# Early transfer of the fourth chunk, a new order on VectorE at the outset, and weight conversion by halves in a fused retention and feed-forward kernel

## The chip, the cores and the metric

The kernel runs on one core of one Trainium2 chip. The metric is the device time of one execution in microseconds (us). A profiled execution gives a trace; its span, from the first to the last instruction, is 1.7 to 2.4 us shorter than the device time of the same run. Engines are called by their short names in the profile: PE is TensorE, PEld its weight loads, DVE is VectorE, ACT is ScalarE, SPq the queue that issues transfers. PSUM is the memory in which this kernel's matmuls leave their results.

## The reference, cut to what matters

```python
# retention: batch 4, 8 heads, 768 tokens, head size 64
state = gamma * state + k_t (outer) v_t
y_t = scale * q_t @ state
x = y as (3072 tokens, 512)
# feed-forward, w_in (512, 2048) and w_out (2048, 512) in 64-bit floats
h = x @ w_in
g = h * erf(softplus(h))
out = g @ w_out
```

The kernel does retention in chunks of 128 tokens (scores, mask, outputs, an addition to the state) and the feed-forward part in 32-bit floats. The weights come as 64-bit floats and are converted on the chip from their bits, piece by piece. There are 16 pieces of 1 MB; a piece of `w_in` serves two of the hidden blocks of the first 512 tokens.

## The kernel before

The first 512 tokens need four chunks. Then hidden blocks (g, u), with g the group and u the block in it, alternate with project(g), which multiplies the gated hidden values by `w_out`. Everything is emitted in program order, and in the traces each engine works through its own instructions in that order.

```python
def load(j):                      # k, q, v of chunk j
    KQ[j] = loads.tile([P, 2, H, D], F32, name="kq")     # pool of three
    V[j] = loads.tile([P, H, D], F32, name="v")
    ...

def conversion(n):                # piece n, five steps, one per yield
    ...
    nc.vector.tensor_scalar(power, hi, 0x7FF00000, None, op0=ALU.bitwise_and)      # mask
    nc.scalar.activation(power, power, AF.Relu, bias=below, scale=8.0)             # ScalarE
    yield
    nc.vector.tensor_scalar(number, hi, 0xFFFFF, 1 << 20, ...)
    yield
    nc.vector.scalar_tensor_tensor(numberf, number, 2.0**32, lo, ...)
    yield
    nc.vector.scalar_tensor_tensor(power, hi, 1 << 31, power, ...)   # needs the Relu
    load_pieces_after(n)
    yield
    nc.vector.scalar_tensor_tensor(to, numberf, 2.0**-52, power, ...)
    done.add(pieces[n])
    yield

def weights():                    # the order of all steps
    before = iter(())
    for n in range(n_p):
        now = conversion(n)
        if n > 1:                 # look ahead: mask and Relu of n before the rest of n - 1
            next(now)
            yield
        for _ in before:
            yield
        before = now
    ...

def pace(n):                      # room is a budget: one step for each unit
    room += n
    while room >= 1:
        next(weight_steps, None)
        room -= 1

def need(*what):                  # emit steps until this weight is there
    while what not in done:
        ...
        room -= 1

def hidden(g, u):
    ft = g * FG + u
    need("in", ft // 2)
    ...                                            # 4 matmuls (8 in the trace) into PSUM tile p
    nc.scalar.copy(HS[g][:, ...], p)               # ScalarE
    done.add(("hidden", ft))
    pace_around(3.4)                               # steps of the conversion come here
```

The gate of group g, two table loads and two activations over 2048 columns, is 6.4 us on ScalarE and follows hidden (g, 3).

## Time and profile before

| stage of the kernel before (span 694.0 us) | us | PE busy | DVE busy | granted PE clock |
|---|---|---|---|---|
| four chunks of retention, 0 to 33 | 33.0 | 25.83 | 16.92 | 0.95 |
| hidden blocks (0,0) to (1,3), 33 to 67 | 34.0 | 32.59 | 32.20 | 1.00 |
| project(0) to project(2), 67 to 140 | 73.0 | 73.00 | 60.11 | 1.00 |
| the remaining tokens, 140 to 694 | 554.0 | 548.40 | 274.59 | 1.00 |

Device time was 694.71 us when the prediction was made (three runs, 694.33 to 694.75). The profiled run took 695.74. The table is summed from windows of the trace: busy time of an engine in a stretch, and the share of its full clock that TensorE was granted. PE is full from 67 to 140 us, and the change is aimed at what lies before, so only the first two rows have something to give, 7.2 + 1.4 us of PE's idle time (the last row has 5.6 us more).

### The profile page before, as it was taken

To read this page: it belongs to the slowest core of one execution; us is meant where nothing else is said; L and a number is where in the kernel's file an instruction comes from. 1 tells how busy PE (TensorE), PEld (TensorE's weight loads), DVE (VectorE), ACT (ScalarE), POOL (GpSimd) and SP (SyncE) were. 2 spreads that over 40 slices of the span, in tenths; PEclk is the share of its full clock that TensorE was granted. 3 is DMA by queue.
4 is the path that set the end of the run, shared out by engine and by line. 5 is a ranking of instruction groups with operands and counts; after the bars stand their busy time and mean duration, and the time that the engine had idled before them with its cause. 6 is when DMAs were issued, how large, how long until landed. Compare 5 with 4: busy or idle time off the path is not lost.

```text
span 694.0 us, 14331 instructions
## 1 busy us (share of the span) xinstructions
PE 679.8 (98%) x6214; PEld 579.7 (84%) x6214; DVE 383.8 (55%) x581; ACT 257.2 (37%) x291; POOL 6.6 (1%) x21
## 2 busy tenths in 40 slices
PE   8799999999999999999999999999999999999997
PEld 7544454486999999999999999999999999999996
DVE  4599999364863663564455455544544554343323
ACT  3266453425244143243342341441441432432440
POOL 2000000010000000000000000000000000000000
PEclk9999999999999999999999999999999999999999
DMA  9999963102321231222222222322311200000000
GB/s 191 209 254 246 208 167 91 31 1 37 104 45 32 68 56 30 63 45 44 68 43 44 69 39 46 71 37 44 70 39 39 54 30 1 2 31 2 1 31 32
DMA packets 147216, 47.12 MB, mean 68 GB/s; under 512 B 135760, under 2 KB 136016, under 8 KB 147152
## 3 DMA queue, kind: packets, MB, share of 16 engines
q1 hardware_dynamic: 144640, 45.66, 30.0%
q8 instruction: 49, 0.80, 0.5%
q10 hardware_dynamic: 2512, 0.53, 0.5%
q14 instruction: 15, 0.12, 0.1%
HBM read 39.86 MB, written 6.29 MB: 67 GB/s over the span
## 4 chain that ended last, share of the span: by engine, by line
PE 91%; DVE 3%; DMA 2%; SPq 1%; issue 1%; ACT 0%; POOL 0%; DVEq 0%; POOLq 0%
PE hp L712 36%; PE o L784 35%; PE o L655 8%; PE hp L642 4%; DMA w_in_sb<-in_moe_w_in_dram 2%; PE r L520 1%; PE hp L485 1%; PE o L367 1%; PE o L556 1%; SPq L114 1%; DMA w_out_sb<-in_moe_w_out_dram 1%; DVE w_out_sb L211 1%; PE hp L535 1%; PE r L408 1%; PE r L535 1%
## 5 line engine op out<-in xcount | busy, mean ns | idle before, releaser
L712 PE MATMUL hp<-xs,w_in_sb 128*128 128x128 f32 x1280 | 149.8, 275 | 0.0
L712 PEld LDWEIGHTS hp<-xs,w_in_sb 128*128 128x128 f32 x1280 | 147.8, 192 | 1.6 <-issue 0.5
L784 PE MATMUL o<-w_out_sb,h 128*128 128x256 f32 x640 | 141.7, 379 | 0.0
L784 PEld LDWEIGHTS o<-w_out_sb,h 128*128 128x128 f32 x640 | 121.6, 190 | 16.5
L712 PE MATMUL hp<-xT,w_in_sb 128*128 128x128 f32 x960 | 113.7, 275 | 0.0
L712 PEld LDWEIGHTS hp<-xT,w_in_sb 128*128 128x128 f32 x960 | 111.9, 192 | 1.9 <-issue 1.0
L784 PE MATMUL o<-w_out_sb,e 128*128 128x256 f32 x480 | 112.1, 383 | 0.0
L631 DVE TENSOR_TENSOR e<-h,e 128x1024 f32<-128x1024 f32 x42 | 49.6, 1221 | 102.5 <-ACT e L612 102.5
L784 PEld LDWEIGHTS o<-w_out_sb,e 128*128 128x128 f32 x480 | 88.2, 190 | 11.6
L642 PE MATMUL hp<-xT,w_in_sb 128*128 128x512 f32 x128 | 56.5, 595 | 0.5 <-ACT xT L475 0.5
L737 DVE TENSOR_TENSOR h<-h,hp 128x512 f32<-128x512 f32 x20 | 13.8, 688 | 75.3 <-PE hp L712 75.3
L607 ACT ACT_TABLE_LOAD x24 | 30.8, 1283 | 60.8 <-issue 45.3
L642 PEld LDWEIGHTS hp<-xT,w_in_sb 128*128 128x128 f32 x128 | 23.9, 190 | 29.2 <-issue 28.2
L612 ACT ACTIVATE e<-e 128x2048 f32<-128x2048 f32 (+1 forms) x23 | 42.2, 1838 | 0.2
L607 ACT ACTIVATE e<-h 128x2048 f32<-128x2048 f32 x22 | 42.1, 1912 | 0.2
L725 DVE TENSOR_TENSOR h<-h,hp 128x512 f32<-128x512 f32 x20 | 13.8, 688 | 51.3 <-PE hp L712 51.3
L735 ACT COPY h<-hp 128x512 f32<-128x512 f32 x20 | 11.7, 587 | 60.2 <-PE hp L712 60.2
L730 ACT COPY h<-hp 128x512 f32<-128x512 f32 x20 | 11.7, 587 | 57.9 <-PE hp L712 57.9
L728 ACT COPY h<-hp 128x512 f32<-128x512 f32 x20 | 11.7, 587 | 55.3 <-PE hp L712 55.3
L612 ACT ACT_TABLE_LOAD x24 | 30.8, 1283 | 0.4
L574 ACT COPY xT<-r 128x256 f32<-128x256 f32 x32 | 10.5, 375 | 54.8 <-PE r L520 54.8
L723 ACT COPY h<-hp 128x512 f32<-128x512 f32 x20 | 11.8, 589 | 48.6 <-PE hp L712 48.6
(123 smaller groups left out, 676.5 us busy)
## 6 DMA issues: line engine op xcount, KB each, us to landing
w_out_sb<-in_moe_w_out_dram SPq DMA_DIRECT2D x14, 512.0 KB, 5.1
kq<-in_k_dram SPq DMA_DIRECT2D x24, 256.0 KB, 3.7
v<-in_v_dram SPq DMA_DIRECT2D x24, 256.0 KB, 3.1
w_in_sb<-in_moe_w_in_dram SPq DMA_DIRECT2D x12, 512.0 KB, 8.7
out_dram<-r SPq DMA_DIRECT2D x23, 256.0 KB, 3.3
kq<-in_q_dram SPq DMA_DIRECT2D x256, 16.0 KB, 1.8
kb<-in_k_dram SPq DMA_DIRECT2D x256, 16.0 KB, 1.7
w_out_sb<-in_moe_w_in_dram SPq DMA_DIRECT2D x4, 512.0 KB, 7.8
```

What stands on the lines that cost most here:

```text
L535: nc.tensor.matmul(other[a][own, u % 2, D:] if crossed else pp[a][own, u % 2, t], V[j][t, 2 * u + r, :], AM[j][t, r, u, :D], start=crossed ...
L607: nc.scalar.activation(E[g], HS[g], AF.Softplus)
L612: nc.scalar.activation(E[g][:, half], E[g][:, half], AF.Erf)
L631: nc.vector.tensor_tensor(E[g][:, half], HS[g][:, half], E[g][:, half], op=ALU.mult)
L642: nc.tensor.matmul(p, w_in_of(ft, kk), XC[0][:, kk, :], start=(kk == 0), stop=(kk == n_k - 1))
L655: nc.tensor.matmul(O[0][tt].rearrange("p (d c) -> p d c", d=2), E[g][:, u * TCH + tt * P : u * TCH + (tt + 1) * P], w_out_of(ft), start=(f ...
L712: nc.tensor.matmul(bank[:, u, :], w_in_sb[:, s, IN[a], kk, u * P : (u + 1) * P], XS[m][b][:, kk, :], start=(p in (1, 2, 5) and u == 0 and ...
L723: nc.scalar.copy(h["11"], flat)
L725: nc.vector.tensor_tensor(h["11"], h["11"], flat, op=ALU.add)
L728: nc.scalar.copy(h["12"], flat)
L737: nc.vector.tensor_tensor(h["12"], h["12"], flat, op=ALU.add)
L784: nc.tensor.matmul(O[m][i][:, half, :], G[g][a][:, u * P : (u + 1) * P], w_out_sb[:, s, OUT[b], u, :], start=i not in started, stop=(s == ...
```

## The change

It has three parts. The fourth chunk (j = 3) no longer waits for one of three buffers; its place is the tile of the first gate, which isn't written for a long time yet. VectorE scales the next chunk before it masks the present one now for the third chunk too (for the first two it did already), and hardly any weights are converted during the chunks. The first two pieces are converted in two halves each, so that the first hidden block needs half a piece only. Along with these, looking ahead starts later (`n > 3`), the budget starts at 0, and the fifth chunk's steps move one hidden block later.

```diff
 def load(j):
+    if j == JPC - 1:
+        x = act.tile([P, N], F32, name="e", bufs=1)     # the first gate's place
+        KQ[j] = x[:, : 2 * d_model]...
+        V[j] = x[:, 2 * d_model : 3 * d_model]...
+    else:
         ...
+    if j == JPC - 1:
+        load_piece(0)                                   # between q and v of chunk 3
...
 def conversion(n):
+    for part in range(2) if n < 2 else (None,):         # halves for pieces 0 and 1
         mask; Relu
-        yield
+        if part is None:
+            yield
         number
         yield
         ...
...
-            if n > 1:
+            if n > 3:
                 next(now)
                 yield
...
-load(1); load(2); load_piece(0)
+for j in range(1, JPC): load(j)
+for n in range(1, 4): load_piece(n)
...
 def hidden(g, u):
-    need("in", ft // 2)
+    need("in", ft)
...
+for j in range(JPC):
+    S_(j)                               # scores
+    if j + 1 < JPC: K_(j + 1)           # scale the next chunk
+    if j: A(j - 1)                      # state
+    if j + 1 < JPC: T(j + 1)            # transposes
+    else: next(weight_steps)
+    M(j)                                # mask
+    O_(j)                               # outputs
 early = False
+room = 0.0
```

More of the change, by code (lines that the diff above doesn't have):

```diff
@@ L101, in load @@
         b, c = divmod(j, NC)
-        KQ[j] = loads.tile([P, 2, H, D], F32, name="kq")
-        V[j] = loads.tile([P, H, D], F32, name="v")
+        if j == JPC - 1:
+            x = act.tile([P, N], F32, name="e", bufs=1)
+            KQ[j] = x[:, : 2 * d_model].rearrange("p (i h d) -> p i h d", i=2, h=H)
+            V[j] = x[:, 2 * d_model : 3 * d_model].rearrange("p (h d) -> p h d", h=H)
+        else:
+            KQ[j] = loads.tile([P, 2, H, D], F32, name="kq")
+            V[j] = loads.tile([P, H, D], F32, name="v")
         now = slice(c * C, (c + 1) * C)
@@ L139 @@
     raws = [x[:, : 2 * CE].bitcast(I64) for x in spare]
-    number = spare[0][:, 2 * CE :].bitcast(U32)
+    numbers = spare[0][:, 2 * CE :].bitcast(U32)
     powers = [x[:, 2 * CE :].bitcast(U32) for x in spare[1:3]]
@@ L169, in load_piece @@
                 )
-    held = []
     def load_pieces_after(n):
@@ L176, in load_pieces_after @@
             if place[later] == place[n]:
-                if early:
-                    held.append(later)
-                else:
-                    load_piece(later)
+                load_piece(later)
                 break
-    def load_held():
-        for n in held:
-            load_piece(n)
-        held.clear()
     def conversion(n):
         which, i = pieces[n]
-        words = raws[place[n]].bitcast(U32).rearrange("p (n w) -> p n w", w=2)
-        lo, hi = words[:, :, 0], words[:, :, 1]
@@ L195, in conversion @@
         half, s, at = i // 4, i % 4 // 2, i % 2
-        if which == "in":
-            to = w_in_sb[:, s, 2 * half : 2 * half + 2, :, at * 2 * P : (at + 1) * 2 * P]
-            form, sizes = "p (d k f) -> p d k f", dict(d=2, k=2)
-        else:
-            to = w_out_sb[:, s, 2 * half : 2 * half + 2, at * 2 : at * 2 + 2, :]
-            form, sizes = "p (d f c) -> p d f c", dict(d=2, f=2)
-        power = powers[n % 2]
-        nc.vector.tensor_scalar(power, hi, 0x7FF00000, None, op0=ALU.bitwise_and)
@@ L204, in conversion @@
-        nc.scalar.activation(power, power, AF.Relu, bias=below, scale=8.0)
-        yield
-        nc.vector.tensor_scalar(
-            number, hi, 0xFFFFF, 1 << 20, op0=ALU.bitwise_and, op1=ALU.bitwise_or
-        )
-        yield
-        numberf = number.bitcast(F32)
-        nc.vector.scalar_tensor_tensor(numberf, number, 2.0**32, lo, op0=ALU.mult, op1=ALU.add)
-        yield
-        nc.vector.scalar_tensor_tensor(
-            power, hi, 1 << 31, power, op0=ALU.bitwise_and, op1=ALU.bitwise_or
-        )
@@ L216, in conversion @@
-        load_pieces_after(n)
-        yield
-        nc.vector.scalar_tensor_tensor(
-            to,
-            numberf.rearrange(form, **sizes),
-            2.0**-52,
-            power.bitcast(F32).rearrange(form, **sizes),
-            op0=ALU.mult,
-            op1=ALU.mult,
-        )
-        done.add(pieces[n])
-        yield
+        for part in range(2) if n < 2 else (None,):
+            words = raws[place[n]].bitcast(U32)
+            if which == "in":
+                f = slice(at * 2 * P, (at + 1) * 2 * P)
+                if part is not None:
+                    f = slice((at * 2 + part) * P, (at * 2 + part + 1) * P)
+                to = w_in_sb[:, s, 2 * half : 2 * half + 2, :, f].rearrange("p d k f -> p (d k) f")
+            else:
+                to = w_out_sb[:, s, 2 * half : 2 * half + 2, at * 2 : at * 2 + 2, :].rearrange(
+                    "p d f c -> p d (f c)"
+                )
+            words = words.rearrange("p (a b w) -> p a b w", a=to.shape[1], w=2)
+            number, power = (
+                x.rearrange("p (a b) -> p a b", a=to.shape[1]) for x in (numbers, powers[n % 2])
+            )
+            if part is not None:
+                f = slice(part * P, (part + 1) * P)
+                words, number, power = words[:, :, f], number[:, :, f], power[:, :, f]
+            lo, hi = words[:, :, :, 0], words[:, :, :, 1]
+            nc.vector.tensor_scalar(power, hi, 0x7FF00000, None, op0=ALU.bitwise_and)
+            nc.scalar.activation(power, power, AF.Relu, bias=below, scale=8.0)
+            if part is None:
+                yield
+            nc.vector.tensor_scalar(
+                number, hi, 0xFFFFF, 1 << 20, op0=ALU.bitwise_and, op1=ALU.bitwise_or
+            )
+            yield
+            numberf = number.bitcast(F32)
+            nc.vector.scalar_tensor_tensor(numberf, number, 2.0**32, lo, op0=ALU.mult, op1=ALU.add)
+            if part is None:
+                yield
+            nc.vector.scalar_tensor_tensor(
+                power, hi, 1 << 31, power, op0=ALU.bitwise_and, op1=ALU.bitwise_or
+            )
+            if part != 0:
+                load_pieces_after(n)
+            yield
+            nc.vector.scalar_tensor_tensor(
+                to, numberf, 2.0**-52, power.bitcast(F32), op0=ALU.mult, op1=ALU.mult,
+            )
+            done.update((which, 2 * i + u) for u in (range(2) if part is None else (part,)))
+            yield
@@ L294 @@
     nc.scalar.copy(idle_out, ident[:, :1])
-    load(1)
-    load(2)
-    load_piece(0)
+    for j in range(1, JPC):
+        load(j)
+    for n in range(1, 4):
+        load_piece(n)
     causal = const.tile([P, C], F32, name="causal")
@@ L581, in sub_visit @@
             nc.vector.tensor_tensor(state, state, new[1], op=ALU.add)
-    def ret_loads(j):
-        if j == 0:
-            load(j + 3)
-        if j < 3:
-            load_piece(j + 1)
     def ret_add(j):
@@ L651, in project @@
             O[0] = [ps_o.tile([P, d_model], F32, name=f"o{i}") for i in range(TT)]
-        need("out", 2 * g + 1)
+        need("out", g * FG + FG - 1)
         for u in range(FG):
@@ L835 @@
     keep_warm(3)
-    n_first = JPC
-    for j in range(n_first):
+    for j in range(JPC):
         S_(j)
-        ahead = j < 2
-        if ahead:
+        if j + 1 < JPC:
             K_(j + 1)
+        if j:
+            A(j - 1)
+        if j + 1 < JPC:
             T(j + 1)
+        else:
+            next(weight_steps)
         M(j)
         O_(j)
-        if not ahead and j + 1 < n_first:
-            K_(j + 1)
-            T(j + 1)
-        ret_loads(j)
-        if j == 1:
-            A(j)
-            room = 1.0
-        pace(1)
-        if j != 1 and j + 1 < n_first:
-            A(j)
     early = False
-    load(JPC)
-    load_held()
-    waiting.append((A, n_first - 1))
+    room = 0.0
+    waiting.append((A, JPC - 1))
     after = [
-        [([], []), ([], []), ([], []), ([], [(K_, 4)])],
+        [([], []), ([(load, 4)], []), ([], []), ([], [])],
         [
-            ([(load, 5)], []),
+            ([(load, 5)], [(K_, 4)]),
+            ([], []),
             ([(T, 4)], []),
             ([(S_, 4)], [(M, 4)]),
-            ([(O_, 4), (load, 6)], [(A, 4), (K_, 5)]),
         ],
         [
-            ([], []),
+            ([(O_, 4), (load, 6)], [(A, 4), (K_, 5)]),
             ([(T, 5), (load, 7)], []),
```

## The prediction

> **What bounds the kernel now.** I read the page first (busy shares), then the windows, then the chain of waits up to 70 us, then the timelines of VectorE (DVE), ScalarE (ACT) and the DMA queue for the stretch in which TensorE (PE) is not full.
>
> The page and the windows (PE busy, PEld, DVE, ACT, POOL, granted clock, DMA share, GB/s):
>
> ```profile
> PE 679.8 (98%) x6214; PEld 579.7 (84%) x6214; DVE 383.8 (55%) x581; ACT 257.2 (37%) x291; POOL 6.6 (1%) x21
> ...
> 20.00:25.00 5.00, 2.33 (x44) 1.84 (x44) 4.97 (x7) 1.15 (x1) 0.00 (x0) 0.94 0.94 202
> 25.00:30.00 5.00, 3.82 (x44) 3.19 (x44) 2.56 (x4) 1.82 (x4) 0.00 (x0) 0.72 1.06 220
> ...
> 60.00:67.00 7.00, 5.62 (x57) 3.11 (x55) 6.93 (x9) 1.74 (x2) 0.00 (x0) 1.00 0.84 264
> 67.00:140.00 73.00, 73.00 (x221) 33.66 (x220) 60.11 (x64) 34.51 (x34) 0.00 (x0) 1.00 0.54 129
> ```
>
> PE idles 694.0 - 679.8 = 14.2 us in all, and from 67 to 140 us not at all. A faster outset can give at most a few us of 694; a new wait of PE in the first 140 us adds in full.
>
> Where the outset is lost (VectorE, then PE):
>
> ```profile
> 19.94 0.69 DVE L203 TENSOR_SCALAR w_out_sb<-w_out_sb 128x1024 uint32<-128x1024 uint32 x1
> ...
> 22.41 0.68 DVE L433 TENSOR_TENSOR am<-r,causal 128x512 f32<-128x512 f32 x1
> ...
> 24.74 1.22 DVE L393 TENSOR_TENSOR kq<-kq,kq_s 128x1024 f32<-128x1024 f32 x1
> ...
> 33.03 20.87 PE L642 MATMUL hp<-xT,w_in_sb 128*128 128x512 f32 x48 [0.47 <-ACT xT L475]
> ```
>
> The conversion of weight piece 0 goes ahead of the third mask (19.94 to 22.41), so PE stands still for 2.5 us (20.64 to 23.15); the clock is then 0.5 for 3.4 us (24.25 to 27.7 in half-us windows). The fourth chunk is scaled at 24.74, as its load was issued only when chunk 0's buffer came free (13.58). The hidden matmuls begin at 33.03 and run without a hole; project(0) begins at 67.01.
>
> The lines on which my prediction turns are these of ScalarE:
>
> ```profile
> 40.20 0.59 ACT L645 COPY h<-hp 128x512 f32<-128x512 f32 x1 [2.85 <-PE hp L642]
> 40.68 1.15 ACT L204 ACTIVATE w_in_sb<-w_in_sb,below 128x1024 uint32<-128x1024 uint32 x1
> ```
>
> VectorE's mask for that Relu ended at 40.26 and ScalarE had been idle 2.85 us, yet the Relu began only at 40.68, behind the copy of hidden block 1, because it stands behind it in the program. Here it costs nothing: it is for piece 3, two blocks early.
>
> **What the Trainium skill says.** (1) "PSUM — Partial Sum Buffer", section "Engine vs sequencer instructions": the queues of ScalarE and VectorE are strict FIFO. The two lines above agree (0.42 us of needless waiting). (2) "ScalarE: Activation LUTs", "What ACT_TABLE_LOAD costs": an ACTIVATE with a pointer bias takes about 280 ns + 0.833 ns per element: 1.13 us for 1024 (trace 1.15), so I take 0.71 for a half of 512. (3) "VectorE: DVE Perf Modes", "The TRN2 errata — SBUF-src ops pay a fixed extra latency per instruction": (N+151)/0.96 ns in fp32: 1.22 us for 1024 (trace 1.22), so 0.69 for 512. (4) "TensorE: Matmul & The Clock Gate", "What's actually happening": after an idle window of about 3.4 us TensorE gets half its clock. The trace agrees (0.5 for 3.4 us), and shows that a window with 28% PE work (0.94 of 3.4 us from 20.84) is idle enough.
>
> **The change part by part.**
>
> *Fourth chunk early.* The loads are the same bytes, no longer waiting for a buffer. Their order puts k and q of chunk 3 at 2.88 MB of the stream; by the windows (129, 220, 214, 199 GB/s) 2.8 MB are in at 15 us, so about 16 us, before VectorE wants it (16). Piece 0 ends at 3.9 MB (21 us), v at 4.2 (22), piece 1 at 5.2 (27), piece 2 at 6.3 (33): all in time.
>
> *VectorE's order.* No conversion before the third mask, and K and T of the next chunk go ahead of the mask. Then a chunk is scores 1.1 + two masks 1.3 + outputs 2.1 = 4.5 us instead of 5.4 and then about 7. From the end of O(0) at 13.56: O(1) 18.1, O(2) 22.7, S(3) 23.8, mask until 25.5 (held 0.3 by half a conversion step), O(3) 26.7, copies 0.6. Piece 0's first block needs three half operations after the mask, 25.5 + 2.0. So the first hidden block starts near 27.5 instead of 33.0: **-5.5 us**, the dip of the clock included.
>
> *Fifth chunk's steps one block later.* M(4) now runs beside project(0). In the kernel before, 33.03 to 67.01 are 33.98 us with 8 hidden blocks of 3.43, T 0.87, S 1.09 and O 2.15 in them, 31.57 us of work; the rest, **2.4 us** around 63 to 65, is the wait for that mask, and goes.
>
> *Conversion by blocks, without looking ahead.* I followed the counter "room" through the listing. It starts at 0; each wanted step takes 1 and each block gives 3.4. Before hidden(0,0) only the first half of piece 0 is converted. The second half's Relu is emitted after hidden(0,0)'s copy (room reaches only 0.99..), the halves of piece 1 after the copies of (0,1) and (0,2), piece 2's after (0,3)'s, piece 3's (behind piece 4's) after (1,1)'s, piece 5's after (1,3)'s. The kernel before began piece n+1's Relu before it finished piece n from the start; now this holds from piece 4 on only. But the very next block needs that weight. So PE ends block e, and waits for copy, Relu, two VectorE operations. From e, copy ends and Relu begins at +0.79 (0.31 to the copy, 0.48 to the next, both in the trace):
> - half piece: 0.79 + 0.71 + 0.05 + 0.69 + 0.02 + 0.69 + 0.05 = 3.0 us, three times (before blocks (0,1), (0,2), (0,3)) = 9.0
> - piece 2 before (1,0): 0.79 + 1.15 + 0.05 + 1.22 + 0.02 + 1.23 + 0.05 = 4.5
> - piece 3 before (1,2): the same with piece 4's Relu in front (1.05) = 5.6
> - project(0,0) wants pieces 4 and 5. From the end of piece 3 VectorE has gated(0) 2.3, piece 4's last four steps and piece 5's five, piece 6's mask: about 12.2 us, against 8.8 us of PE (two blocks, T, S): 3.4.
>
> Together **+22.5 us**. Sum: -5.5 - 2.4 + 22.5 = +14.6: 694.7 + 14.6 = 709.3 at full clock.
>
> *The clock.* Each of these waits falls on the 3.4 us windows at an unknown phase. A wait of 3.0 us leaves 12% of a window busy when it lies fully in one, one of 4.5 or 5.6 us nearly always spoils one. A spoiled window halves the clock of the next and loses up to 1.7 us. Two to five of six waits: **+3 to +8**, I take 4. So about 713.
>
> **The rivals.**
>
> A, *the gain stays*: the Relu isn't held by the copy, or the weights come ahead, and only the outset counts: 694.7 - 7.9 = 687. For it: the change is meant so, and VectorE's mask and number are early in any case. Against it: the two ScalarE lines, and the Relu's result is an input of the operation that the block waits for. I see no step that emits it earlier.
>
> B, *VectorE is the bound*: without ScalarE's waits VectorE would have, from the third mask at 25.5, 33 to 34 us of conversions, gated(0) and scaling until piece 5 is done, so project(0) at 59 instead of 58: 689. It speaks for it that VectorE is 6.93 of 7 us busy before 67. With the waits of PE, VectorE has holes instead, and this stays only as the last term.
>
> C, *DMA is the bound*: piece 5 is behind 10.2 MB, some 48 us; VectorE wants it at 46 in A, at 70 in my story. It would add 2 to 3 us to A (690) and nothing to mine.
>
> D, *clock at full throughout* with shorter waits, some hidden in the end of a block: 704 to 709.
>
> **Range and chances.** My sum is 713; without the clock 709, with each wait spoiling a window and a late start 721. The range 702 to 721 leaves a tenth for A to C and a tenth for each kind of surprise at its edges. 2% slower is 708.6. Slower 0.74, same 0.24 (A, B, C, and short waits), faster 0.02: under 680.8 all of PE's idle time would have to go.
>
> **What would show it.** The first line of L642 at 27 to 28 us (outset right). Then L642 must no longer be one group of 48 without a hole but four blocks with holes of about 3, 3, 3, 4.5, and 5.6 before (1,2), each put down to VectorE's third operation (w_in_sb), and on ScalarE L645's copy directly ahead of each Relu. project(0) near 79 or later instead of 67, the fifth chunk's O behind it. PE busy in work the same, so PE's idle time about 14 us more; granted clock 0.5 to 0.9 in several windows from 31 to 80 us, and 1.0 after. From project(0) on the two kernels should run alike. I am wrong if L642 runs on without holes from 28 us: then it is A or B, 687 to 690; wrong in size if the holes are there but the clock is 1.0.

## The result, and the profile after

The changed kernel took 714.9 us (median of four runs: 712.75, 713.36, 716.44 and 718.02), the kernel before 694.68 (four runs, 694.33 to 694.75). The ratio is 1.0296, with a 95% interval of 1.0251 to 1.034. The profiled run is the fastest one; its span is 711.0 us.

First the windows of the changed kernel (columns: PE, PEld, DVE, ACT, POOL busy, granted clock, DMA share, GB/s):

```profile
0.00:28.00 28.00, 23.76 (x310) 21.09 (x310) 14.40 (x26) 8.71 (x19) 3.50 (x16) 1.00 1.10 201
28.00:85.00 57.00, 37.18 (x93) 16.02 (x94) 32.81 (x42) 21.33 (x25) 0.00 (x0) 0.88 0.66 152
85.00:157.00 72.00, 72.00 (x258) 33.74 (x257) 63.43 (x68) 33.92 (x35) 0.00 (x0) 1.00 0.57 138
```

The outset is shorter and has its clock, 28 us at 1.00 against 33 at 0.95. Between the first hidden block and project(0) PE is busy 37.18 of 57.00 us, and the clock is 0.88. VectorE has as much work there as before (32.81 against 32.20 us), spread over 57 us in place of 34. From 85 us on PE is full again.

PE's timeline says where the holes are (start, duration, group of instructions, and in brackets PE's idle time before it and what ended it):

```profile
28.35 3.67 PE L643 MATMUL hp<-xT,w_in_sb 128*128 128x512 f32 x8 [0.68 <-DVE w_in_sb L229]
34.87 3.67 PE L643 MATMUL hp<-xT,w_in_sb 128*128 128x512 f32 x8 [2.84 <-DVE w_in_sb L229]
41.38 3.67 PE L643 MATMUL hp<-xT,w_in_sb 128*128 128x512 f32 x8 [2.84 <-DVE w_in_sb L229]
47.89 3.67 PE L643 MATMUL hp<-xT,w_in_sb 128*128 128x512 f32 x8 [2.84 <-DVE w_in_sb L229]
55.90 9.42 PE L643 MATMUL hp<-xT,w_in_sb 128*128 128x512 f32 x16 [4.34 <-DVE w_in_sb L229]
70.69 5.43 PE L643 MATMUL hp<-xT,w_in_sb 128*128 128x512 f32 x8 [5.37 <-DVE w_in_sb L229]
...
84.67 5.85 PE L656 MATMUL o<-w_out_sb,e 128*128 128x512 f32 x13 [1.24 <-DVE w_out_sb L229]
```

The kernel before had one group of 48 matmuls here. Now each of the first four blocks stands alone behind a hole, and every hole was ended by L229, VectorE's last step of a conversion. The starts of the first four are 6.5 us apart where 3.43 is the work. The fifth and sixth block last 9.42 us, where 16 such matmuls at full clock take 7.10 (experiment 2), and the seventh 5.43.

VectorE's timeline says what L229 waited for, by the step ahead of it (L223, the one that takes the Relu's result):

```profile
33.30 0.69 DVE L223 SCALAR_TENSOR_TENSOR w_out_sb<-w_out_sb 128x512 uint32<-128x512 uint32 x1 [3.35 <-ACT w_out_sb L212]
...
68.06 1.23 DVE L223 SCALAR_TENSOR_TENSOR w_in_sb<-w_in_sb 128x1024 uint32<-128x1024 uint32 x1 [7.98 <-ACT w_in_sb L212]
```

VectorE, not PE alone, stood still: 3.35 us in one case, 7.98 in the other, both times for ScalarE's L212, the Relu. ScalarE's timeline closes the loop:

```profile
32.06 0.59 ACT L646 COPY h<-hp 128x512 f32<-128x512 f32 x1 [3.69 <-PE hp L643]
32.54 0.72 ACT L212 ACTIVATE w_out_sb<-w_out_sb,below 128x512 uint32<-128x512 uint32 x1
```

ScalarE had been idle for 3.69 us when the copy of hidden block (0,0) could start at last, and the Relu for block (0,1) is the instruction behind it. Its mask had been ready since 28.9 us. So PE waits for VectorE, VectorE for ScalarE, ScalarE for PE: the block that needs the weight is held until the block before it has been copied.

The ledger of the profiled run, taken from start to start:

| term | predicted, us | in the trace, us | from |
|---|---|---|---|
| first hidden block earlier | -5.5 | -4.7 | 33.03 to 28.35 |
| wait around 63 to 65 us gone | -2.4 | -2.4 | 33.98 of which 31.57 is work, in the kernel before; 1.4 of it is PE's wait for the mask |
| three holes for halves | +9.0 | +9.2 | starts 6.52, 6.51 and 6.51 apart, less 3.43 each |
| hole for piece 2 | +4.5 | +4.6 | 55.90 - 47.89 - 3.43 |
| hole for piece 3 | +5.6 | +5.6 | 70.69 - 55.90 - 6.87 - 2.3 of half clock |
| hole at project(0) | +3.4 | +1.5 | it begins at 81.45, goes on at 84.67 after four matmuls of 1.7 in all |
| half clock | +4 | +4.1 | 9.42 - 7.10, and 5.43 - 3.6 |
| sum | +18.6 | +17.9 | |

The span grew by 17.0 us, 0.9 less. PE's idle time in the last 554 us is 5.6 us in the kernel before and 4.3 in the changed one, 1.3 less, which covers the rest. I did not follow where in those 554 us it lies. The medians are 20.2 us apart, 3.2 more than the two spans: the profiled run of the kernel before took 695.74 us, above its other runs, and that of the changed kernel was its fastest.

### The profile page after: what moved, and what is told of

It reads as the page before. It is cut to its first block, busy times and chain, and to the rows that moved or that the text cites. A ratio compares the mean times of both kernels' runs of the same rounds, so it can differ in the third digit from the quotient of the medians. Undisturbed runs are those within 1.5% of the kernel's fastest.

```text
span 711.0 us, 14343 instructions
## 1 busy us (share of the span) xinstructions
PE 682.6 (96%) x6214; PEld 579.0 (81%) x6214; DVE 385.2 (54%) x591; ACT 257.4 (36%) x293; POOL 6.6 (1%) x21
## 4 chain that ended last, share of the span: by engine, by line
PE 92%; DVE 2%; DMA 2%; SPq 1%; ACT 1%; issue 1%; DVEq 0%
PE hp L713 35%; PE o L785 34%; PE hp L643 8%; PE o L656 8%; PE r L527 1%; PE hp L492 1%; DMA e<-in_q_dram 1%; PE o L563 1%; SPq L119 1%; SPq L122 1%; DMA w_out_sb<-in_moe_w_out_dram 1%; DVE w_in_sb L229 1%; PE r L415 1%; PE hp L542 1%; DVE w_in_sb L223 1%
## 5 line engine op out<-in xcount | busy, mean ns | idle before, releaser
L643 PE MATMUL hp<-xT,w_in_sb 128*128 128x512 f32 x128 | 61.6, 632 | 18.9 <-DVE w_in_sb L229 18.9
L646 ACT COPY h<-hp 128x512 f32<-128x512 f32 x16 | 9.4, 587 | 67.7 <-PE hp L643 67.7
L736 ACT COPY h<-hp 128x512 f32<-128x512 f32 x20 | 11.7, 587 | 60.2 <-PE hp L713 60.2
L731 ACT COPY h<-hp 128x512 f32<-128x512 f32 x20 | 11.7, 586 | 57.9 <-PE hp L713 57.9
L729 ACT COPY h<-hp 128x512 f32<-128x512 f32 x20 | 11.7, 587 | 55.3 <-PE hp L713 55.3
```

The costliest lines, as they stand in the source:

```text
L643: nc.tensor.matmul(p, w_in_of(ft, kk), XC[0][:, kk, :], start=(kk == 0), stop=(kk == n_k - 1))
L729: nc.scalar.copy(h["12"], flat)
L731: nc.scalar.copy(h["22"], flat)
L736: nc.scalar.copy(h["21"], flat)
```

## The experiments

**The theory.** The Relu of a piece is emitted behind the copy of the block just before the one that needs the piece; ScalarE keeps its order, so each such piece costs a hole, and the holes take TensorE's clock down. **The rivals.** 1: the halves give VectorE more to do than it can. 2: the pieces land too late, because the fourth chunk's bytes are now ahead of them. Kernels were compared with the kernel before on the same chip in the same rounds; its median was 694.7 us in experiments 1 to 8 and 695.4 in 9 and 10. All results were correct. When two profiled runs are compared, note that the first hidden block alone begins between 27.62 and 30.10 us in the seven with the early chunk, the new order and halves.

### 1. The budget starts at 6

```diff
-    room = 0.0
+    room = 6.0
```

> One number: the counter starts at 6 instead of 0 after the fourth chunk, so that the same conversion steps stand several blocks earlier in the program; no step, transfer or half is added or removed. Theory (a Relu stands behind the copy of the block just before the one that needs it): the holes before hidden(0,2), (0,3), (1,0) and (1,2) go, the one of 2.8 us before (0,1) stays, first block still near 28.4 us, project(0,0) between 60 and 63 us, total 689 to 693 us. Rival 1 (VectorE has too much to do in half pieces): no VectorE work is removed, so the total stays over 705. Rival 2 (pieces land too late behind the fourth chunk): the steps would wait for transfers instead, total over 705.

Measured: 695.64 us (695.31 to 696.22), ratio 1.0013 (0.9998 to 1.0028). One number gives back nearly all of the 20 us, with the same halves and the same transfers, so both rivals fall, at least as the cause of the 20 us. The size was 2.6 us over the top of what I expected. PE's timeline has the one hole that was foreseen and another one that wasn't:

```profile
35.51 19.10 PE L643 MATMUL hp<-xT,w_in_sb 128*128 128x512 f32 x40 [2.84 <-DVE w_in_sb L229]
57.42 3.70 PE L643 MATMUL hp<-xT,w_in_sb 128*128 128x512 f32 x8 [2.81 <-ACT h L646]
```

The 40 matmuls take 19.10 us where five blocks of 3.43 are 17.2; between 34 and 40 us the clock was 0.72. One hole of 2.84 us was enough for that here. The second hole is of another kind: block (1,2) waits for ScalarE to copy a bank of PSUM, and ScalarE is in the first gate, which two Relus emitted earlier have put off.

### 2. Mask and Relu ahead of the copy in the first four blocks

```diff
     ...                                   # matmuls of hidden (g, u)
+    if g == 0:
+        next(weight_steps)
+        room -= 1
     nc.scalar.copy(HS[g][:, ...], p)
```

> In the first four hidden blocks the next piece's mask and Relu are emitted ahead of the block's copy instead of behind it; the counter pays for it, nothing else. Theory: the three holes of 2.84 and the one of 4.34 us before hidden(1,0) go, with the half clock around the latter (about 2.4 us); the one before (1,2) stays or grows by about 1 us (its Relu is still emitted behind the first gate and the copies): total 696 to 701 us. Rival 1 and 2 (VectorE's work, late transfers): the holes stay, over 710.

Measured: 699.6 us (697.63 to 700.95), ratio 1.0071 (1.0045 to 1.0097), as expected. Only places in the order changed. PE's timeline:

```profile
28.77 13.97 PE L647 MATMUL hp<-xT,w_in_sb 128*128 128x512 f32 x32 [0.68 <-DVE w_in_sb L229]
43.65 7.10 PE L647 MATMUL hp<-xT,w_in_sb 128*128 128x512 f32 x16 [0.90 <-DVE w_in_sb L229]
56.12 5.84 PE L647 MATMUL hp<-xT,w_in_sb 128*128 128x512 f32 x8 [5.37 <-DVE w_in_sb L229]
```

The first four blocks are one group of 32 matmuls without a hole. The hole before (1,0) is 0.90 in place of 4.34; the one before (1,2), whose Relu I left where it was, is 5.37 to the digit.

### 3. Looking ahead from the third piece on

```diff
-            if n > 3:
+            if n > 1:
```

> Only the condition for looking ahead goes back from 'from the fifth piece on' to 'from the third piece on'. Theory: the holes before hidden(0,1), (0,2), (0,3) stay at 2.8 us each (the halves get no look ahead in either); the hole before (1,0) shrinks from 4.3 to some 1.5 us (VectorE's four steps then count, not ScalarE) and that before (1,2) goes, with most of the half clock: total 697 to 703 us. Rival 1 and 2: over 710.

Measured: 705.78 us (704.64 to 707.26), ratio 1.0159 (1.0143 to 1.0176), 3 us over the top of the range. PE waited for L229 four times, 10.2 us in all: 2.84, 3.87 and 2.84 before the three halves, and 0.68 before the first block. The holes before (1,0) and before (1,2) for a piece are gone, as the theory has it. What I had not counted is that piece 2's Relu, now looked ahead for, stands before that of the second half hole (3.87 in place of 2.84), and two dips of the clock (0.50 at 44 to 46 and again at 51 to 53 us): the third block lasts 5.37 us in place of 3.67, and the next three together 12.09, which have 10.5 at full clock. A wait of 1.73 us for the copy behind the gate came new. So this line is the part of the change that costs two of the six holes; the halves, which get no look ahead, cost three.

### 4. Budget at 6, and the Relu for block (0,1) ahead of the first copy

```diff
+    if g == 0 and u == 0:
+        next(weight_steps)
+        room -= 1
     nc.scalar.copy(HS[g][:, ...], p)
...
-    room = 0.0
+    room = 6.0
```

> The counter starts at 6 and the mask and Relu of the second half of piece 0 are emitted ahead of the first hidden block's copy. Theory: hidden runs from about 28.4 us without a hole up to project(0,0), where VectorE is now the later one by 1 to 3 us: total 688 to 692 us, faster than both kernels. Rival 1 and 2: over 705.

Measured: 692.22 us (690.97 to 693.99), ratio 0.9965 (0.9943 to 0.9986): a little faster than the kernel before. The one step emitted earlier (mask, Relu and number of that half) is the whole difference from experiment 1, 3.4 us by the medians. In the profiled runs the way from the first hidden block to project(0) falls from 37.45 to 33.37 us: the hole of 2.84 us and its dip of 1.9 go, less some 0.7 of new small waits. PE's waits from 27 to 62 us (us in total, times, longest):

```profile
PE hp L647 <- ACT h L653: 2.9, 1, 2.9
PE hp L647 <- DVE w_in_sb L229: 1.0, 2, 0.7
```

The weights cost 1.0 us; what is left is the gate's hole before (1,2).

### 5. The changed kernel with its waits filled

```diff
+    WARM = {(0, 1): 11, (0, 2): 11, (0, 3): 11, (1, 0): 18, (1, 2): 22}
 def hidden(g, u):
     need("in", ft)
+    keep_warm(WARM.get((g, u), 0))        # matmuls of the identity into an idle bank
```

> The changed kernel with matmuls of the identity into the idle bank in the five waits of the hidden blocks (11, 11, 11, 18 and 22 of them, some 0.2 us each, shorter than each wait). No wait of the weights is removed. Theory (the waits cost 17 us by themselves and the halved clock adds some 4 us more in the profiled run, more in the slowest runs): granted clock 1.0 in all stretches from 28 us on, total 706 to 710 us and its runs within 2 us of each other, where those of the changed kernel spread over 5. Rival (the clock takes no part, or is a result of something else): unchanged at 712 to 718.

Measured: 708.58 us, four runs: 710.4, 708.59, 708.57, 708.52; ratio 1.0198 (1.0181 to 1.0215). The useful work and its waits are the same; PE only does something idle in between. The windows of its profiled run from 30 to 82 us:

```profile
30.00:82.00 52.00, 49.07 (x238) 31.23 (x238) 31.95 (x40) 20.34 (x24) 0.00 (x0) 1.00 0.68 158
```

The clock is 1.00 there, and the mean of the runs falls from 715.1 to 709.0 us. So the halved clock costs 6 us on average, of some 20. (Where the runs that weren't profiled lost their clock isn't on record; part of it may lie before the hidden blocks.) The spread of the changed kernel's runs goes with the clock: they have a mean clock of 0.990, 0.990, 0.988 and 0.986 in the order of their times, and three of the four here have 1.000. The fourth (710.4, clock 0.997) is the profiled one; it lost its clock from 22 to 26 us, before the hidden blocks.

### 6. Whole pieces in place of halves

Experiment 4 with this:

```diff
-        for part in range(2) if n < 2 else (None,):
+        for part in (None,):
...
-            if n > 3:
+            if n > 1:
...
     if g == 0 and u == 0:
-        next(weight_steps)
-        room -= 1
+        for _ in range(2):
+            next(weight_steps)
+        room -= 2
```

> The version with the counter at 6, with whole pieces in place of halves and looking ahead from the third piece on as in the kernel before; two steps are emitted ahead of the first copy. It keeps the early fourth chunk and the order. Theory (what the halves give at the first block is taken back at project(0), which VectorE sets): first hidden block near 31 us, 2.7 later than with halves, but project(0) near 61 to 62 us all the same: total 690.5 to 694 us. Rival (the halves are what makes the gain): the full 2.7 us later, 694.5 to 696.

Measured: 696.14 us (695.44 to 696.87), ratio 1.0019 (1.0004 to 1.0034). My expectation was wrong and the rival nearly right: with whole pieces the time is 3.9 us over that of experiment 4 (the look ahead differs too, as the diff shows). The first block did begin near 31 us, but PE's timeline shows what I had not counted:

```profile
31.16 10.07 PE L647 MATMUL hp<-xT,w_in_sb 128*128 128x512 f32 x16 [3.01 <-DVE w_in_sb L229]
```

PE stands 3.01 us for the conversion of the whole piece, and loses its clock: the windows have 0.50 from 31 to 37 us, and the first two blocks take 10.07 us in place of 7.10. The halves save the wait and with it the dip.

### 7. The fifth chunk's transposes in the gate's hole

Experiment 4 with this:

```diff
         ([(load, 5)], [(K_, 4)]),
-        ([], []),
         ([(T, 4)], []),
+        ([], []),
         ([(S_, 4)], [(M, 4)]),
```

> The version with the counter at 6 and the Relu ahead of the first copy, with the fifth chunk's transposes moved from behind hidden(1,2) to ahead of it, into the 2.9 us in which TensorE waits for the first gate to let ScalarE copy a bank free. Theory: the 0.87 us of transposes move into that hole, project(0) begins 0.5 to 0.9 us earlier unless VectorE's piece 5 sets it: total 690.5 to 692.5 us. Rival (VectorE sets project(0) whatever TensorE does): unchanged within 0.3 us of that version's 692.2.

Measured: 690.91 us (six runs, 689.65 to 692.77), ratio 0.9948 (0.993 to 0.9965). This is the fastest version, half a per cent below the kernel before and 3.4% below the changed one (690.91 / 714.9 = 0.966). Against experiment 4 it gains 1.3 us by the medians; the two intervals overlap, so take the sign from the trace: project(0) begins at 59.87 us instead of 61.32, of which 0.33 was there at the first hidden block already, so 1.1 us are the gate's hole. PE's waits from 27 to 60 us:

```profile
PE hp L647 <- DVE w_in_sb L229: 1.0, 2, 0.7
PE r L415 <- DVE kq L400: 0.9, 1, 0.9
PE hp L647 <- ACT h L653: 0.7, 1, 0.7
```

The gate's hole is 0.7 us in place of 2.9. VectorE is busy for 31.55 of the 33 us from 27 to 60, so it may set this stage now; no run tests that.

### 8. The fourth chunk late again

Experiment 4 with chunk 3 in the pool of three, behind piece 0, so that its transfer waits for chunk 0's buffer:

```diff
-        if j == JPC - 1:                    # the first gate's place
+        if False:
...
-        if j == JPC - 1:
-            load_piece(0)
         nc.sync.dma_start(V[j], ...)
+        if j == JPC - 2:
+            load_piece(0)
```

> The version with the counter at 6 and the Relu ahead of the first copy, but with the fourth chunk in the pool of three as before, behind piece 0, so that its transfer waits for chunk 0's buffer. Theory (the early transfer and the order need each other: the order asks for the chunk at 16 us): scaling of chunk 3 begins near 21 us in place of 18.5, the first hidden block near 30.5, total 693.5 to 696. Rival (the order alone gives the gain): within 0.5 us of 692.2.

Measured: 698.52 us (697.31 to 699.44), ratio 1.0052 (1.0037 to 1.0067), 2.5 us over the range. VectorE's timeline:

```profile
22.36 1.23 DVE L400 TENSOR_TENSOR kq<-kq,kq_s 128x1024 f32<-128x1024 f32 x1 [6.74 <-DMA kq<-in_q_dram]
```

VectorE waits 6.74 us for q of the fourth chunk. PE stands too, its clock is 0.50 from 23 to 29 us, and the first hidden block is at 34.46. I had the wait (it came 1.4 us later than I said) and not the clock. With the new order the early transfer, and its place ahead of piece 0, is worth 6.3 us (698.52 - 692.22).

### 9. The early fourth chunk alone, in the kernel before

```diff
-    KQ[j] = loads.tile(...); V[j] = loads.tile(...)
+    if j == JPC - 1: x = act.tile([P, N], F32, name="e", bufs=1); KQ[j], V[j] = parts of x
+    else: KQ[j] = loads.tile(...); V[j] = loads.tile(...)
...
-load(1); load(2); load_piece(0)
+load(1); load(2); load(3)                    # piece 0 between q and v of chunk 3
+for n in range(1, 4): load_piece(n)
...
-    ret_loads(j)                             # chunk 3 and pieces 1 to 3, in the loop
```

> The kernel before with the early transfer of the fourth chunk alone (into the first gate's place, pieces 1 to 3 behind it), everything else as it was. Theory: VectorE doesn't come to chunk 3 before 24.7 us for its own order, so nothing is gained; piece 0 lands some 2 us later and holds the third mask by up to 1 us: total 694.3 to 696.5. Rival (the transfer itself is what shortens the outset): 690 to 692.

Measured: 696.46 us (695.86 to 697.57), ratio 1.0014 (1.0001 to 1.0028). Nothing is gained, as expected: VectorE comes to chunk 3 at 28.48 us only, behind the third mask and piece 0, which landed for it at 23.68. I had let piece 0 hold the third mask by up to 1 us; it begins at 26.15 in place of 22.41, and the first hidden block of the profiled run at 38.05 in place of 33.03. So the early transfer alone makes the outset longer (the clock was halved from 22.9 to 36.5 us); part of this is made up for later, as the span is 1.9 us longer. Of the two parts that shorten the outset neither does it alone: experiment 8 has the order without the transfer, this one the transfer without the order.

### 10. The fifth chunk's steps one block later, alone, in the kernel before

```diff
-    [([], []), ([], []), ([], []), ([], [(K_, 4)])],
+    [([], []), ([], []), ([], []), ([], [])],
     [
-        ([(load, 5)], []),
+        ([(load, 5)], [(K_, 4)]),
+        ([], []),
         ([(T, 4)], []),
         ([(S_, 4)], [(M, 4)]),
-        ([(O_, 4), (load, 6)], [(A, 4), (K_, 5)]),
     ],
     [
-        ([], []),
+        ([(O_, 4), (load, 6)], [(A, 4), (K_, 5)]),
```

> The kernel before with the fifth chunk's steps one block later, alone. Theory: the wait for the fifth chunk's mask around 63 to 65 us goes (2.4 us with its ends), but project(0) then comes to where piece 5's conversion ends (63.5 us), so 1 to 2 us remain: total 692.5 to 694. Rival (the wait only moves): 694.3 to 695.

Measured: 695.62 us (695.09 to 697.25), ratio 1.0009 (0.9996 to 1.0022). The rival was right: the wait only moves. One line of PE's timeline in the kernel before, then one in this run:

```profile
64.26 0.43 PE L456 MATMUL r<-qT,state 64*64 64x128 f32 x2 [1.21 <-DVE am L433]
56.06 3.70 PE L642 MATMUL hp<-xT,w_in_sb 128*128 128x512 f32 x8 [1.09 <-ACT h L645]
```

After the first hidden block PE waits 1.1 us for the copy behind the gate, where the kernel before has 1.4 us (1.21 and 0.17) for the mask. The transposes of chunk 4 had stood between blocks (1,1) and (1,2) and covered the end of the gate; moved behind (1,2) they uncover it. Experiment 7 is the same finding from the other side.

## Why the prediction was right, point by point

**The bound.** That PE's idle time at the outset was all there was to win, and that a new wait of PE before 140 us would add in full, held: from 85 to 157 us the changed kernel's PE is full, and after that it idles no longer than before.

**The outset.** It came 0.8 us later than predicted (28.35 against 27.5). The term that was off is the landing of chunk 3: "so about 16 us" from bytes and rates. VectorE's timeline of the changed kernel says 18.57 us, and that VectorE waited:

```profile
18.57 1.23 DVE L400 TENSOR_TENSOR e<-e,kq_s 128x1024 f32<-128x1024 f32 x1 [2.89 <-DMA e<-in_q_dram]
```

In the eight traces whose instructions are the same up to there (the changed kernel and experiments 1 to 7) it began between 17.61 and 19.22 us, each time right after this wait; so the landing varies by 1.6 us from run to run.

**The holes.** This step carried the prediction. The order was followed by hand through the budget, the sizes were sums of durations, and the trace has them within 0.1 us for five of six. The two formulas of the Trainium skill that gave the half sizes held: by "ScalarE: Activation LUTs", section "What ACT_TABLE_LOAD costs", an estimate of 0.71 us for an ACTIVATE of 512 elements, 0.72 in the trace; by "VectorE: DVE Perf Modes", section "The TRN2 errata — SBUF-src ops pay a fixed extra latency per instruction", whose formula is for an addition of two tensors, an estimate of 0.69 for 512 elements, 0.69 in the trace for the conversion's operations. Experiments 1, 2 and 4 show the cause: with the steps that hold the Relu earlier in the order and nothing else changed, the holes go; VectorE's part of these steps was early in any case (the mask at 28.9 us). One reading of the prediction is loose: the kernel before looks ahead from piece 2 on (`n > 1`), not "from the start".

**The hole at project(0)** was given 3.4 us and measured 1.5. I let it wait for pieces 4 and 5 both. Its first four matmuls (as the trace counts) need piece 4 only and ran before the hole, 1.7 us. Two things left out nearly cancel: VectorE stood 1.86 us for piece 5's Relu, again behind a copy, and the half clock stretched PE's work before project(0) by 1.8.

**The clock** was given 4 us, from 3 to 8; the profiled run lost 4.1, and experiment 5 puts the average at 6. The median of 714.9 against 713 fits this: the profiled run, for which the sum holds best, took 712.75. That the 4 was met is in part luck. I let a spoiled wait cost up to 1.7 us, in two to five of six waits; two were spoiled and cost 2.3 and 1.8, because the clock was at 0.50 for 6.8 us each time (53.75 to 60.6 and 67.4 to 74.2), twice the window of 3.4, with PE back at work within the first (55.90 and 70.69).

**The wait around 63 us.** Counting 2.4 us off is right as a difference of two timelines in which six other waits come new. To call all of it the wait for the mask was not: PE waits 1.4 us for it, and the rest lies in small gaps. As a gain of that part it is wrong: alone it gives nothing (experiment 10), as the first gate's copy takes its place.

**The rivals.** A (the gain stays) and B (VectorE is the bound) were rejected for the changed kernel and are what one sees with the order mended: experiment 7 is at 690.9, where A said 687 and B 689. C (DMA) shows only in the landing of chunk 3. D (full clock, 704 to 709) is experiment 5, 708.6.

**What the rest of the experiments adds.** The idea of the change was sound: early transfer and order together shorten the outset, and halves avoid a wait of 3 us. What turned a gain of 2.5 us (experiment 4) into a loss of 20 was the pacing that came with it: the budget of 0, which alone makes 19 us of it (experiment 1), and the second half's Relu behind the first copy. The later look ahead costs 9 us while the budget is 0 (experiment 3); experiment 4 keeps it and is faster than the kernel before.

## What to carry to other kernels

When work for one engine is cut finer so that its user can start sooner, look at each helper engine that it passes: an instruction that stands behind a consumer's own copy in a queue can't run before that consumer has finished, however early its inputs are. Follow the emission order of the next step on that engine before counting the gain, and emit the helper's step ahead of the copy. Then add the clock to the price: here the halved clock added 4 to 6 us to some 21 us of holes.

## What the Trainium skill lacked or had wrong

- "TensorE: Matmul & The Clock Gate", section "HAM oscillation — how this bites in real kernels", gives as a rule that there should be no idle gap of PE over about 3.4 us. Shorter ones were enough here: 2.5 us in the kernel before (0.50 afterwards), 2.84 us in experiment 1 (0.72 from 34 to 40 us), 3.01 us in experiment 6 (0.50 from 31 to 37). In the changed kernel three holes of 2.84 us in a row kept the clock at 1.00. That fits the windows of fixed length of the section "What's actually happening"; the rule doesn't say it.
- The same page doesn't say how much work makes a window count as busy. Ten traces here have a dip; counted in windows of 3.41 us from its start, the clock was lost after windows in which PE was busy for 0 to 1.33 us (39%), and in the outset of experiment 5 after one of 1.65 us with small matmuls; other windows of 1.53 us (45%) and more kept it. To get it back took more: after windows begun at half clock with up to 2.79 us of work (82%, experiment 9) it stayed at half. This is read from the traces and was not tested.
- No page says how much the landing of a transfer deep in a full queue varies from run to run: here by 1.6 us for chunk 3 (VectorE began on it between 17.61 and 19.22 us in eight traces, each time right after waiting for it).
